# Attention and feed-forward on one core: the add that builds x moves to the next slot, loads run further ahead, and five engines follow a written order

## The chip, the cores and the metric

The kernel runs on one core of a Trainium2 chip. The metric is the device time of one execution in microseconds; lower is better. The profile is that of one execution of its own. Its engines are called PE (TensorE, matmuls), DVE (VectorE), ACT (ScalarE), POOL (GpSimd) and SP (SyncE); the last two issue most of the DMAs.

## The reference

Two layers, one behind the other. The first is attention over q, k, v of shape (8, 8, 576, 64): batches, heads, tokens, head dimension. Each head's output is the sum of a coarse part and a local part:

```python
q_d = q.reshape(B, H, Sd, 4, D).mean(axis=3)        # k_d, v_d likewise
out_d = sm_attn(q_d, k_d, v_d)                      # softmax attention over 144 pooled tokens
out_up = np.repeat(out_d, 4, axis=2)
mask = np.abs(pos[:, None] - pos[None, :]) < 4      # each token sees 3 neighbours on each side
out_local = softmax(where(mask, scale * q @ k.T, -1e9)) @ v
attn_out = out_up + out_local
```

Heads are then put side by side, which gives x with 8 * 576 = 4608 tokens of 512 numbers. The second layer is a gated feed-forward block with d_ff = 1536:

```python
out = (np.maximum(x @ w_gate, 0) * (x @ w_val)) @ w_out
```

Inputs and output are float32 in memory. The kernel converts to float16 while loading and adds up matmuls in float32.

## The kernel before, in words

The work is cut in two ways. Attention goes by **pairs** of heads of one batch: 32 pairs `hp`, four to a batch. Feed-forward goes by **chunks** of 512 tokens: nine chunks `c`. A chunk needs the x of all four pairs of the batches that it touches, so chunk c can be complete once pair 4c+3 is.

A loop over **slots** `s` from -5 to 35 ties the two together. Slot s does attention for pair hp = s + 5 and a quarter of the feed-forward of chunk s // 4: three blocks `emit_h` (128 columns of d_ff each) and, from slot 4 on, one block `emit_y` (128 tokens of output) of the chunk before. Slots below 0 hold attention alone, slots from 28 on almost feed-forward alone. Four more `emit_y` end the program.

The helpers, with what they issue:

- `emit_load(hp)`: POOL issues six DMAs from memory, two each for q, k and v of a pair, into rings of NL = 5 buffers (`q16`, `k16`, `vw`); the first and the last pair have their v in more pieces.
- `emit_wslice`, `emit_wo`: POOL issues slices of the three weight matrices, in slots -4 to 3.
- `emit_qkT(hp)`: SP issues two transposing DMAs, q16 to `qT` and k16 to `kT` (rings of 3).
- `emit_pool(hp)`: two DVE reductions, the sums of four tokens of qT and kT (L179).
- `emit_s1(hp)`: scores on PE (L203 coarse, L218 local), exponentials on ACT (L226, L235), the band masks on DVE (L238).
- `emit_vd(hp)`: pooled v on PE (L188), copied by DVE (L195).
- `emit_s2(hp)`: the products with v on PE (L254, L266), their division by the row sums on DVE (L274 to L285) into `xo`; SP then transposes `xo` to `xoT` by DMA (L291), and DVE adds the coarse part, repeated four times, to the local part and writes `xT` (L292).
- `emit_h(c, jj)`: eight matmuls of 512 columns (L308), Relu on ACT, the product `gT` on DVE (L318). The first four matmuls take one quarter of x each, which is one pair's heads.
- `emit_y(c, ty)`: twelve matmuls (L324), a copy on ACT and the DMA to memory.

All matmul results share one ring of eight PSUM banks. In `with tc.manual_schedule(engines={PE})` only PE follows the program's text as its order. The order of the instructions on DVE, ACT, SP and POOL, their DMAs included, is set ahead of time by a planner from its own cost estimates; each engine then works through its list in order, waiting where an input or a buffer isn't ready. In the trace the planner's list on DVE for a slot is: the add to xT for the pair of the slot before, the masks and the two reductions mixed, the first gT, the output of the next pair, the second gT, the copy of vd, the third gT. On SP the transpose of xo comes first, those of q and k behind it. On POOL it drew some q and k loads ahead of the v loads.

Of the kernel before, what the change touches and what calls it, by code (L numbers as in the profile page):

```python
# [10 lines left out]
FP16 = mybir.dt.float16  # L11
AF = mybir.ActivationFunctionType
ALU = mybir.AluOpType
AX = mybir.AxisListType
PE = mybir.EngineType.PE


def _np_constants():
# [28 lines left out]
def kernel(  # L47
# [44 lines left out]
    def ring(n, shape, dtype, name):  # L92
        return [keep.tile(shape, dtype, name=f"{name}{i}") for i in range(n)]

    NL = 5
    q16 = ring(NL, [96, NB, 128], FP16, "q16_")
    k16 = ring(NL, [96, NB, 128], FP16, "k16_")
    vw = ring(NL, [128, 2, NB, 65], FP16, "vw_")
    qT = ring(3, [128, S], FP16, "qT_")
    kT = ring(3, [128, KW], FP16, "kT_")  # L100
    qd = ring(2, [128, SD], FP16, "qd_")
    kd = ring(2, [128, SD], FP16, "kd_")
    ee = ring(2, [128, 2, S + 32], FP16, "ee_")
    ed = ring(2, [72, 2, 2 * SD + 64], FP16, "ed_")
    vd = ring(2, [72, 2, 2, 65], FP16, "vd_")
    xo = ring(2, [96, NB + 2, 128], FP16, "xo_")
    xoT = ring(2, [128, NB + 2, 96], FP16, "xoT_")
    xT = keep.tile([128, NPB, NTOK], FP16, name="xT")

    for t in kT:  # L110
# [51 lines left out]
                )  # L162

    def emit_qkT(hp):
        r, r3 = hp % NL, hp % 3
        nc.sync.dma_start_transpose(
            out=qT[r3].rearrange("p (j t) -> p j t", j=NB),
            in_=q16[r].rearrange("p j c -> p (j c)"),
        )
        nc.sync.dma_start_transpose(  # L170
            out=kT[r3][:, KPAD : KPAD + S].rearrange("p (j t) -> p j t", j=NB),
            in_=k16[r].rearrange("p j c -> p (j c)"),
        )

    def emit_pool(hp):
        r3, r2 = hp % 3, hp % 2
        with nc.allow_low_precision(reason="4:1 pooling sum"):
            for src, dst in ((qT[r3][:, :], qd[r2]), (kT[r3][:, KPAD : KPAD + S], kd[r2])):
                nc.vector.tensor_reduce(  # L179
                    out=dst, in_=src.rearrange("p (t f) -> p t f", f=4), axis=AX.X, op=ALU.add  # L180
                )
# [13 lines left out]
        nc.vector.tensor_copy(out=vd[hp % 2], in_=ps[0:72, :, :, :])  # L195

    def emit_s1(hp):
        r3, r2 = hp % 3, hp % 2
        sd_ps = [psum.tile([72, 2, SD], FP32, name="sd_ps", tag="bank") for _ in range(2)]
        for c in range(2):  # L200
            for hh in range(2):
                lo = 64 * hh
                nc.tensor.matmul(  # L203
                    out=sd_ps[hh][:, c, :],
                    lhsT=kd[r2][lo : lo + 64, bass.ts(c, 72)],
                    rhs=qd[r2][lo : lo + 64, :],
                    start=True,
                    stop=True,
                )
        sc_ps = []  # L210
        for g in range(2):
            pair = [psum.tile([128, 3, NQ], FP32, name="sc_ps", tag="bank") for _ in range(2)]
            sc_ps.append(pair)
            for jj in range(3):
                j = 3 * g + jj
                for hh in range(2):
                    lo = 64 * hh
                    nc.tensor.matmul(  # L218
                        out=pair[hh][:, jj, :],
                        lhsT=kT[r3][lo : lo + 64, NQ * j + KPAD - 3 : NQ * j + KPAD + 125],  # L220
                        rhs=qT[r3][lo : lo + 64, NQ * j : NQ * j + NQ],
                        start=True,
                        stop=True,
                    )
        for hh in range(2):
            nc.scalar.activation(  # L226
                out=ed[r2][:, hh, 0 : 2 * SD],
                in_=sd_ps[hh].rearrange("p c t -> p (c t)"),
                func=AF.Exp,
                scale=scale / 16.0,  # L230
            )
        for g in range(2):
            for hh in range(2):
                o = ee[r2][:, hh, 288 * g : 288 * g + 288]
                nc.scalar.activation(  # L235
                    out=o, in_=sc_ps[g][hh].rearrange("p j t -> p (j t)"), func=AF.Exp, scale=scale
                )
                nc.vector.tensor_tensor(  # L238
                    out=o,
                    in0=o,  # L240
                    in1=masks_sb[:, 3 * g : 3 * g + 3, :].rearrange("p j t -> p (j t)"),
                    op=ALU.mult,
                )

    def emit_s2(hp):
        r2 = hp % 2
        b, kk = hp // NPB, hp % NPB
        x = xo[r2]
        od = psum.tile([128, 2, 2, 65], FP32, name="od_ps", tag="bank")
        for hh in range(2):  # L250
            for tcx in range(2):
                for c in range(2):
                    s0 = c * SD + 72 * tcx
                    nc.tensor.matmul(  # L254
                        out=od[:, hh, tcx, :],
                        lhsT=ed[r2][:, hh, s0 : s0 + 128],
                        rhs=vd[r2][:, c, hh, :],
                        start=(c == 0),
                        stop=(c == 1),
                    )  # L260
        us = []
        for hh in range(2):
            u = psum.tile([128, NB, 65], FP32, name="u_ps", tag="bank")
            us.append(u)
            for j in range(NB):
                nc.tensor.matmul(  # L266
                    out=u[:, j, :],
                    lhsT=ee[r2][:, hh, NQ * j : NQ * j + 128],
                    rhs=vw[hp % NL][:, hh, j, :],
                    start=True,  # L270
                    stop=True,
                )
        rd = small.tile([72, 2, 2], FP32, name="rd", tag="rd")
        nc.vector.reciprocal(out=rd, in_=od[0:72, :, :, 64])  # L274
        for hh in range(2):
            nc.vector.tensor_tensor(
                out=x[0:72, NB : NB + 2, 64 * hh : 64 * hh + 64],
                in0=od[0:72, hh, :, 0:64],
                in1=_sap(rd, (0, 72), 2 * hh, [[1, 2], [0, 64]]),
                op=ALU.mult,  # L280
            )
        for hh in range(2):
            ru = small.tile([96, NB], FP32, name="ru", tag="ru")
            nc.vector.reciprocal(out=ru, in_=us[hh][0:96, :, 64])
            nc.vector.tensor_tensor(  # L285
                out=x[:, 0:NB, 64 * hh : 64 * hh + 64],
                in0=us[hh][0:96, :, 0:64],
                in1=_sap(ru, (0, 96), 0, [[1, NB], [0, 64]]),
                op=ALU.mult,
            )  # L290
        nc.sync.dma_start_transpose(out=xoT[r2], in_=x.rearrange("p j c -> p (j c)"))  # L291
        nc.vector.tensor_tensor(  # L292
            out=xT[:, kk, b * S : (b + 1) * S].rearrange("p (c t f) -> p c t f", c=2, f=4),
            in0=xoT[r2][:, 0:NB, :].rearrange("p j t -> p (j t)").rearrange(
                "p (c t f) -> p c t f", c=2, f=4
            ),
            in1=_sap(xoT[r2], (0, 128), NB * 96, [[96, 2], [1, 72], [0, 4]]),
            op=ALU.add,
        )
# [37 lines left out]
    def emit_wslice(i):  # L337
        for src, dst in ((moe_w_gate, wg_sb), (moe_w_val, wv_sb)):
            nc.gpsimd.dma_start(
                dst[:, :, 384 * i : 384 * (i + 1)],  # L340
                _dap(src, 384 * i, [[D_FF, 128], [128 * D_FF, 4], [1, 384]]),
            )
# [4 lines left out]
            _dap(moe_w_out, 384 * i * D_MODEL, [[D_MODEL, 128], [128 * D_MODEL, 3], [1, D_MODEL]]),  # L347
        )

    with tc.manual_schedule(engines={PE}):  # L350
        emit_load(0)
        nc.sync.dma_start(masks_sb, masks_dr)
        nc.sync.dma_start(pool_sb, pool_dr)
        emit_load(1)
        emit_load(2)
        emit_qkT(0)
        emit_pool(0)
        for s in range(-LEAD, NCH * 4):
            hp = s + LEAD
            if hp + 3 < NP:  # L360
                emit_load(hp + 3)
            if s < 0:
                if s >= -4:
                    emit_wslice(s + 4)
            elif s < 4:
                emit_wo(s)
            if hp + 1 < NP:
                emit_qkT(hp + 1)
            if hp < NP:
                emit_s1(hp)  # L370
            if s >= 4:
                emit_y(s // 4 - 1, s % 4)
            if hp + 1 < NP:
                emit_pool(hp + 1)
            if s >= 0:
                emit_h(s // 4, 3 * (s % 4))
            if 1 <= hp <= NP:
                emit_s2(hp - 1)
            if s >= 0:
                emit_h(s // 4, 3 * (s % 4) + 1)  # L380
            if hp < NP:
                emit_vd(hp)
            if s >= 0:
                emit_h(s // 4, 3 * (s % 4) + 2)
        for ty in range(4):
            emit_y(NCH - 1, ty)

# [29 lines left out]
```

## Time and profile before

| | |
|---|---|
| median of 3 runs | 424.23 us (422.62 to 426.31) |
| profiled execution | 425.76 us, its span 424.0 us |
| mean granted TensorE clock | 0.987 |
| PE busy | 350.9 us, 83% of the span |
| DVE busy | 229.6 us, 54% |
| ACT busy | 148.0 us, 35% |
| POOL busy | 159.8 us, 38% |
| moved by DMA | 46.36 MB, mean 109 GB/s |

Rows of one digit per slice cut the span into 40 equal parts of 10.6 us; a digit is the busy share in tenths, 9 being 90% or more. A row of the waits reads: engine and line that waited, what it waited for, microseconds in total, number of times, longest. A row of the chain reads: start, duration, what ran; the chain is followed back from the last instruction to whatever released each step. A row of a timeline reads: start, duration, engine, line, operation, output <- inputs, shapes, how many were merged, and in brackets the idle time ahead of it with its releaser. SPq is SP's queue, on which the transposing DMAs are issued; the row's duration there is the issue alone.

### The profile page before, as it was taken

The numbers are of one execution on the slowest core, as the hardware profiler recorded it, in microseconds if no ns is written. First come the engines' busy times: TensorE is split into PE (matmuls) and PEld (weight loads), VectorE is DVE, ScalarE is ACT, GpSimd is POOL, SyncE is SP. The second block draws the span as 40 slices with busy tenths as digits, with TensorE's granted clock in tenths as the row PEclk, the third lists the DMA queues.
The fourth block names the chain that finished last, engine by engine and source line by source line (L and its number), as shares of the span: only waits on it lengthen the run. The fifth ranks groups of instructions, "written<-read, shape, count | busy, mean of one in ns | idle before, by whom it ended". The sixth has DMA issues, their size and how long they took to land.

```text
span 424.0 us, 7217 instructions
## 1 busy us (share of the span) xinstructions
PE 350.9 (83%) x2640; PEld 178.1 (42%) x2640; DVE 229.6 (54%) x588; ACT 148.0 (35%) x337; POOL 159.8 (38%) x229
## 2 busy tenths in 40 slices
PE   0152324977899979997999999999999999999996
PEld 0142212432445535553555445555555544444442
DVE  0364443356677567766777667785876552222320
ACT  1131110432344434443444454444444423323321
POOL 9995656646944444544553544111200000000000
PEclk9999999986999999999999999999999999999999
DMA  8999999999999999999999999869611221001002
GB/s 78 134 173 160 175 171 176 157 156 167 104 155 127 123 130 127 129 124 115 126 132 116 131 122 136 117 105 98 109 45 45 53 54 51 25 26 51 25 26 99
DMA packets 203604, 46.36 MB, mean 109 GB/s; under 512 B 193072, under 2 KB 198960, under 8 KB 203568
## 3 DMA queue, kind: packets, MB, share of 16 engines
q0 software_dynamic: 133584, 20.47, 68.6%
q1 hardware_dynamic: 64800, 15.99, 28.0%
q10 hardware_dynamic: 5184, 9.44, 6.3%
q8 instruction: 21, 0.34, 0.4%
q14 instruction: 15, 0.12, 0.1%
HBM read 41.14 MB, written 9.44 MB: 119 GB/s over the span
## 4 chain that ended last, share of the span: by engine, by line
PE 55%; DMA 26%; DVE 13%; issue 3%; POOL 2%; ACT 0%; DVEq 0%; SPq 0%; POOLq 0%
PE h_ps L308 32%; PE y_ps L324 17%; DMA xoT_109<-xo_107 12%; DMA xoT_108<-xo_106 10%; DVE gT L318 2%; PE u_ps L266 2%; DMA vw_85<-in_v_dram 2%; DVE ee_100 L238 1%; PE vd_ps L188 1%; DMA q_2_77<-in_q_dram 1%; DVE xo_106 L285 1%; DVE xT L292 1%; PE od_ps L254 1%; DMA qT_92<-q_2_77 1%; DVE xo_107 L285 1%
## 5 line engine op out<-in xcount | busy, mean ns | idle before, releaser
L308 PE MATMUL h_ps<-xT,wg_sb 128*128 128x512 f16 x432 | 115.2, 388 | 20.0 <-DVE xT L292 20.0
L308 PE MATMUL h_ps<-xT,wv_sb 128*128 128x512 f16 x432 | 114.1, 387 | 6.1 <-DVE gT L318 6.1
L324 PE MATMUL y_ps<-wo_sb,gT 128*128 128x512 f16 x432 | 98.9, 380 | 0.0
L308 PEld LDWEIGHTS <-wv_sb 128*128 128x128 f16 x432 | 43.0, 100 | 77.3 <-issue 29.4
L324 PEld LDWEIGHTS <-gT 128*128 128x128 f16 x432 | 40.5, 98 | 47.3
L308 PEld LDWEIGHTS <-wg_sb 128*128 128x128 f16 x432 | 39.3, 99 | 42.9 <-issue 6.3
L332 ACT COPY y_sb<-y_ps 128x512 f32<-128x512 f32 x36 | 21.1, 586 | 63.7 <-PE y_ps L324 63.7
L292 DVE TENSOR_TENSOR xT<-xoT_109 128x576 f16<-128x576 f16 x16 | 12.1, 758 | 45.3 <-DMA xoT_109<-xo_107 45.0
L292 DVE TENSOR_TENSOR xT<-xoT_108 128x576 f16<-128x576 f16 x16 | 12.1, 758 | 43.6 <-DMA xoT_108<-xo_106 43.4
L226 ACT ACTIVATE ed_102<-sd_ps 72x288 f16<-72x288 f32 x32 | 11.3, 402 | 36.2 <-PE sd_ps L203 36.2
L235 ACT ACTIVATE ee_101<-sc_ps 128x288 f16<-128x288 f32 x64 | 21.0, 412 | 1.0 <-PE sc_ps L218 1.0
L235 ACT ACTIVATE ee_100<-sc_ps 128x288 f16<-128x288 f32 x64 | 20.7, 413 | 0.0
L226 ACT ACTIVATE ed_103<-sd_ps 72x288 f16<-72x288 f32 x32 | 11.3, 402 | 26.9 <-PE sd_ps L203 26.9
L203 PE MATMUL sd_ps<-qd_96,kd_98 64*72 64x144 f16 x64 | 5.6, 259 | 17.7 <-DVE kd_98 L179 17.7
L128 POOL DMA_DIRECT2D q_0_75<-in_q_dram x14 | 10.5, 760 | 20.8 <-DMA qT_90<-q_0_75 6.5
L285 DVE TENSOR_TENSOR xo_106<-u_ps,ru 96x384 f16<-96x384 f32 x32 | 17.5, 548 | 0.5
L285 DVE TENSOR_TENSOR xo_107<-u_ps,ru 96x384 f16<-96x384 f32 x32 | 17.5, 548 | 0.4
L188 PEld LDWEIGHTS <-pool_sb 128*128 128x128 f16 x192 | 14.6, 104 | 6.5
L128 POOL DMA_DIRECT2D q_1_76<-in_q_dram x14 | 10.3, 742 | 18.5 <-DMA qT_91<-q_1_76 5.4
L238 DVE TENSOR_TENSOR ee_100<-ee_100,masks_sb 128x288 f16<-128x288 f16 x64 | 16.1, 300 | 0.0
L238 DVE TENSOR_TENSOR ee_101<-ee_101,masks_sb 128x288 f16<-128x288 f16 x64 | 16.1, 300 | 0.0
L128 POOL DMA_DIRECT2D q_3_78<-in_q_dram x12 | 8.8, 741 | 18.4 <-DMA qT_92<-q_3_78 6.4
(307 smaller groups left out, 490.7 us busy)
## 6 DMA issues: line engine op xcount, KB each, us to landing
out_dram<-y_sb ACTq DMA_DIRECT2D x36, 256.0 KB, 2.0
wg_sb<-in_moe_w_gate_dram POOLq DMA_DIRECT2D x4, 384.0 KB, 9.7
wv_sb<-in_moe_w_val_dram POOLq DMA_DIRECT2D x4, 384.0 KB, 9.7
wo_sb<-in_moe_w_out_dram POOLq DMA_DIRECT2D x4, 384.0 KB, 9.6
vw_85<-in_v_dram POOLq DMA_DIRECT2D x13, 96.0 KB, 5.9
vw_86<-in_v_dram POOLq DMA_DIRECT2D x13, 96.0 KB, 4.5
vw_87<-in_v_dram POOLq DMA_DIRECT2D x12, 96.0 KB, 4.4
vw_88<-in_v_dram POOLq DMA_DIRECT2D x12, 96.0 KB, 4.3
```

The costliest lines, as they stand in the source:

```text
L128: nc.gpsimd.dma_start(dst[:, :, 64 * hh : 64 * hh + 64], _dap(src, off + hh * S * D, [[D, 96], [NQ * D, NB], [1, D]]),)
L188: nc.tensor.matmul(out=ps[:, c, :, :], lhsT=pool_sb[:, sig, :], rhs=t[:, :, 3 * c + sig, :], start=(sig == 0), stop=(sig == 2),)
L226: nc.scalar.activation(out=ed[r2][:, hh, 0 : 2 * SD], in_=sd_ps[hh].rearrange("p c t -> p (c t)"), func=AF.Exp, scale=scale / 16.0,)
L235: nc.scalar.activation(out=o, in_=sc_ps[g][hh].rearrange("p j t -> p (j t)"), func=AF.Exp, scale=scale)
L238: nc.vector.tensor_tensor(out=o, in0=o, in1=masks_sb[:, 3 * g : 3 * g + 3, :].rearrange("p j t -> p (j t)"), op=ALU.mult,)
L266: nc.tensor.matmul(out=u[:, j, :], lhsT=ee[r2][:, hh, NQ * j : NQ * j + 128], rhs=vw[hp % NL][:, hh, j, :], start=True, stop=True,)
L285: nc.vector.tensor_tensor(out=x[:, 0:NB, 64 * hh : 64 * hh + 64], in0=us[hh][0:96, :, 0:64], in1=_sap(ru, (0, 96), 0, [[1, NB], [0, 64]]), ...
L292: nc.vector.tensor_tensor(out=xT[:, kk, b * S : (b + 1) * S].rearrange("p (c t f) -> p c t f", c=2, f=4), in0=xoT[r2][:, 0:NB, :].rearrang ...
L308: nc.tensor.matmul(out=h, lhsT=w[:, kk, bass.ts(jj, 128)], rhs=xT[:, kk, c * TCH : (c + 1) * TCH], start=(kk == 0), stop=(kk == 3),)
L318: nc.vector.tensor_tensor(out=gt, in0=r1, in1=h2, op=ALU.mult)
L324: nc.tensor.matmul(out=y_ps, lhsT=gts[c, jj][:, bass.ts(ty, 128)], rhs=wo_sb[:, jj, :], start=(jj == 0), stop=(jj == NJJ - 1),)
L332: nc.scalar.copy(out=y_sb, in_=y_ps)
```

## The change

Four things.

1. The add of L292 leaves `emit_s2` for a function of its own, `emit_xadd`, and is emitted one slot later: in slots from 0 on behind the masks and reductions and ahead of the first `emit_h`, in slots below 0 at the slot's end.
2. Loads are emitted four pairs ahead in place of three, q and k transposes two pairs ahead in place of one.
3. Rings grow: q16, k16, vw from 5 to 7, qT and kT from 3 to 4, xo and xoT from 2 to 3.
4. `manual_schedule` takes all five engines, so DVE, ACT, SP and POOL follow the text's order too.

```diff
-    NL = 5
+    NL = 7
-    qT = ring(3, [128, S], FP16, "qT_")
-    kT = ring(3, [128, KW], FP16, "kT_")
+    qT = ring(4, [128, S], FP16, "qT_")
+    kT = ring(4, [128, KW], FP16, "kT_")
-    xo = ring(2, [96, NB + 2, 128], FP16, "xo_")
-    xoT = ring(2, [128, NB + 2, 96], FP16, "xoT_")
+    xo = ring(3, [96, NB + 2, 128], FP16, "xo_")
+    xoT = ring(3, [128, NB + 2, 96], FP16, "xoT_")
...
-        nc.sync.dma_start_transpose(out=xoT[r2], in_=x.rearrange("p j c -> p (j c)"))
+        nc.sync.dma_start_transpose(out=xoT[hp % 3], in_=x.rearrange("p j c -> p (j c)"))
+
+    def emit_xadd(hp):
+        b, kk = hp // NPB, hp % NPB
+        r2 = hp % 3
         nc.vector.tensor_tensor(
             out=xT[:, kk, b * S : (b + 1) * S].rearrange("p (c t f) -> p c t f", c=2, f=4),
...
+    def emit_slot(s):
+        hp = s + LEAD
+        if hp + 4 < NP:
+            emit_load(hp + 4)
+        if s < 0:
+            if s >= -4:
+                emit_wslice(s + 4)
+        elif s < 4:
+            emit_wo(s)
+        if hp + 2 < NP:
+            emit_qkT(hp + 2)
+        if hp < NP:
+            emit_s1(hp)
+        if hp + 1 < NP:
+            emit_pool(hp + 1)
+        if s < 0:
+            if hp >= 1:
+                emit_s2(hp - 1)
+            emit_vd(hp)
+            if hp >= 2:
+                emit_xadd(hp - 2)
+            return
+        if s >= 4:
+            emit_y(s // 4 - 1, s % 4)
+        if hp - 2 < NP:
+            emit_xadd(hp - 2)
+        emit_h(s // 4, 3 * (s % 4))
+        if hp - 1 < NP:
+            emit_s2(hp - 1)
+        emit_h(s // 4, 3 * (s % 4) + 1)
+        if hp < NP:
+            emit_vd(hp)
+        emit_h(s // 4, 3 * (s % 4) + 2)
 
-    with tc.manual_schedule(engines={PE}):
+    with tc.manual_schedule(engines={ET.PE, ET.DVE, ET.Activation, ET.SP, ET.Pool}):
         emit_load(0)
         nc.sync.dma_start(masks_sb, masks_dr)
         nc.sync.dma_start(pool_sb, pool_dr)
         emit_load(1)
+        emit_qkT(0)
         emit_load(2)
-        emit_qkT(0)
+        emit_qkT(1)
         emit_pool(0)
+        emit_load(3)
         for s in range(-LEAD, NCH * 4):
...
-            if hp + 3 < NP:
-                emit_load(hp + 3)
...
-            if hp + 1 < NP:
-                emit_qkT(hp + 1)
...
-            if 1 <= hp <= NP:
-                emit_s2(hp - 1)
...
+            emit_slot(s)
```

The order of PE's instructions is the same in both.

More of the change, by code (lines that the diff above doesn't have):

```diff
@@ L14 @@
 AX = mybir.AxisListType
-PE = mybir.EngineType.PE
+ET = mybir.EngineType
 def _np_constants():
@@ L164, in emit_qkT @@
     def emit_qkT(hp):
-        r, r3 = hp % NL, hp % 3
+        r, r3 = hp % NL, hp % 4
         nc.sync.dma_start_transpose(
@@ L175, in emit_pool @@
     def emit_pool(hp):
-        r3, r2 = hp % 3, hp % 2
+        r3, r2 = hp % 4, hp % 2
         with nc.allow_low_precision(reason="4:1 pooling sum"):
@@ L197, in emit_s1 @@
     def emit_s1(hp):
-        r3, r2 = hp % 3, hp % 2
+        r3, r2 = hp % 4, hp % 2
         sd_ps = [psum.tile([72, 2, SD], FP32, name="sd_ps", tag="bank") for _ in range(2)]
@@ L246, in emit_s2 @@
         r2 = hp % 2
-        b, kk = hp // NPB, hp % NPB
-        x = xo[r2]
+        x = xo[hp % 3]
         od = psum.tile([128, 2, 2, 65], FP32, name="od_ps", tag="bank")
@@ L354 @@
         emit_load(1)
+        emit_qkT(0)
         emit_load(2)
-        emit_qkT(0)
+        emit_qkT(1)
         emit_pool(0)
+        emit_load(3)
         for s in range(-LEAD, NCH * 4):
-            hp = s + LEAD
-            if hp + 3 < NP:
-                emit_load(hp + 3)
[L362 to L366, printed above, removed]
-            if hp + 1 < NP:
-                emit_qkT(hp + 1)
[L369 to L376, printed above, removed]
-            if 1 <= hp <= NP:
-                emit_s2(hp - 1)
[L379 to L384, printed above, removed]
+            emit_slot(s)
         for ty in range(4):
```

## The prediction

> **What bounds the kernel now.** I read the page first: TensorE's busy row by slice, the DMA row, then who waits for whom, then the chain in order of time, then the timelines of the engines at which the chain leaves TensorE.
>
> ```profile
> span 424.0 us, 7217 instructions
> PE   0152324977899979997999999999999999999996
> DMA  8999999999999999999999999869611221001002
> DVE xT L292 <- DMA xoT_109<-xo_107: 45.0, 14, 6.1
> DVE xT L292 <- DMA xoT_108<-xo_106: 43.4, 14, 6.0
> PE h_ps L308 <- DVE xT L292: 20.0, 6, 9.5
> ```
>
> TensorE is full in the second half and nearly empty in the first sixth; VectorE stands 88 us before the add at L292, waiting for the transpose of x. The chain cuts the span into stages:
>
> ```profile
> 29.54 8.61 DMA xoT_108<-xo_106
> 40.54 7.83 DMA xoT_109<-xo_107
> 69.54 2.29 PE h_ps L308 x5
> 117.61 1.24 PE h_ps L308 x5
> 123.78 2.70 PE y_ps L324 x12
> 264.27 2.70 PE y_ps L324 x12
> 273.63 2.70 PE y_ps L324 x12
> 330.50 2.70 PE y_ps L324 x12
> ```
>
> Stage A, to 69.5 us: attention with no feed-forward work. Stage B, 69.5 to 117.6: slots 0 to 3, up to the last weight block of slot 4's first h matmul. Stage C: the rest. An undisturbed slot with y takes 273.63 - 264.27 = 9.36 us, all of it TensorE; without y (2.6) it is 6.8. B should take 4 x 6.8 + 2.6 = 29.8 and takes 48.1: 18.3 lost. In C, the 22 y from 123.78 to 330.50 take 206.7 us where 21 x 9.36 is 196.6: 10.1 lost. Behind that the rows show TensorE without a gap, and the change leaves it alone.
>
> Why A and B lose: VectorE works in order and stops at the add.
>
> ```profile
> 31.85 0.29 DVE L276 TENSOR_TENSOR xo_107<-od_ps,rd 72x128 f16<-72x128 f32 x1
> 38.17 0.76 DVE L292 TENSOR_TENSOR xT<-xoT_108 128x576 f16<-128x576 f16 x1 [6.03 <-DMA xoT_108<-xo_106]
> 38.85 0.28 DVE L276 TENSOR_TENSOR xo_107<-od_ps,rd 72x128 f16<-72x128 f32 x1
> 96.98 0.76 DVE L292 TENSOR_TENSOR xT<-xoT_109 128x576 f16<-128x576 f16 x1 [6.06 <-DMA xoT_109<-xo_107]
> DMA to landing us min/median/max: 2.7/4.6/9.4
> ```
>
> At 31.85 it had begun pair 1's output, and sat 6 us in the middle of it on pair 0's transpose. One round is a transpose, L, plus what VectorE does from the add to the next issue. L is some 8 us beside weight loads, 2.7 with nothing beside it.
>
> **The change, part by part.**
>
> *A: the add leaves the middle of the slot.* Below s = 0 it now ends the slot, for pair hp-2, so two transposes can be in flight. The order differs from 31.85 on. Five more memsets on POOL (0.3 at most each, row below) shift all by about 0.45, an estimate. Pair 1's output needs 40.54 - 38.85 = 1.7 more, so its transpose leaves at 33.5. From then the q and k transposes of the next pairs are the limit; I take 8 us for each transpose in flight here, the 7.83 above. Pair 4's k transpose follows at 33 and lands near 40, so pair 2's output is ready at 42.7. Pair 5's load is now issued at 28.7 to 33.4, lands by 38, is transposed by 46, and pair 3's output is ready at 48.8. Its transpose lands at 56.8; the add takes 0.76. Pair 6's transposes, which the add now stands behind on VectorE, are in by 54.5. First h complete at 57.6, not 69.5: 11.9 us earlier.
>
> *B: weights against the round.* In slots from 0 on the add stands ahead of the first gT and of the output of the next pair, so here one transpose alone is in flight again.
>
> ```profile
> 287.51 0.69 DVE L318 TENSOR_TENSOR gT<-r_3565,h_ps 128x512 f16<-128x512 f16 x1 [0.63 <-PE h_ps L308]
> 289.99 1.21 SPq L291 DMA_TRANSPOSE xoT_109<-xo_107  x1
> 2.12 0.30 POOL L120 MEMSET xo_107<- 32x256 f16 x1
> 28.19 0.79 POOL L339 DMA_DIRECT2D wg_sb<-in_moe_w_gate_dram  x1
> 34.91 0.76 POOL L339 DMA_DIRECT2D wg_sb<-in_moe_w_gate_dram  x1 [0.63 <-DMA wg_sb<-in_moe_w_gate_dram]
> 45.52 0.75 POOL L339 DMA_DIRECT2D wg_sb<-in_moe_w_gate_dram  x1 [0.84 <-DMA wg_sb<-in_moe_w_gate_dram]
> 55.19 0.75 POOL L339 DMA_DIRECT2D wg_sb<-in_moe_w_gate_dram  x1 [0.51 <-DMA wg_sb<-in_moe_w_gate_dram]
> 65.82 0.78 POOL L345 DMA_DIRECT2D wo_sb<-in_moe_w_out_dram  x1
> 74.54 0.75 POOL L345 DMA_DIRECT2D wo_sb<-in_moe_w_out_dram  x1
> 82.57 0.75 POOL L345 DMA_DIRECT2D wo_sb<-in_moe_w_out_dram  x1
> 93.54 1.66 POOL L159 DMA_DIRECT2D vw_86<-in_v_dram  x2 [4.05 <-PE u_ps L266]
> 95.18 0.75 POOL L345 DMA_DIRECT2D wo_sb<-in_moe_w_out_dram  x1
> wo_sb<-in_moe_w_out_dram POOLq DMA_DIRECT2D x4, 384.0 KB, 9.6
> ```
>
> From gT to the issue is 289.99 - 287.51 = 2.5 us; with the add a round is L + 3.2. Four rounds from 56.8 at L = 8.3 (weights are loading throughout) end at 103. That isn't what decides: slot 4's y needs the last slice of wo. POOL issues weights at a pace set by their own landing (each wg waits for the wg before it), and now puts one pair more ahead of each. So the first slice moves from 28.2 to 33.4; at the old steps of 6.7, 10.6, 9.7, 10.6, 8.7 and 8.0, and 8.5 in place of 12.6 since the 4.05 us wait for u goes with seven buffers, the last leaves at 96.2 and lands at 106. Three matmuls of y and three of h (0.22 each) come before the fourth: 107.3. So 10.3 of the 11.9 remain at the end of B.
>
> POOL's and SP's orders change too. SP now issues a q and k transpose ahead of x's, so a late load would hold x's back; pair 7's would be in flight when pair 4's x goes out at 60, which could make that L 10 to 12. The 3 us by which the round beats the weights cover it. The fourth q, k buffer and third x buffer only take waits away.
>
> *C: two opposite terms.* The stalls at the start of a chunk and those between are different things.
>
> ```profile
> 199.65 0.38 PE L308 MATMUL h_ps<-xT,wg_sb 128*128 128x512 f16 x1 [1.88 <-DVE xT L292]
> 282.41 0.32 PE L203 MATMUL sd_ps<-qd_96,kd_98 64*72 64x144 f16 x4
> 283.36 1.30 ACT L235 ACTIVATE ee_100<-sc_ps 128x288 f16<-128x288 f32 x4
> 285.51 1.03 PE L308 MATMUL h_ps<-xT,wg_sb 128*128 128x512 f16 x4
> 286.13 0.74 DVE L179 TENSOR_REDUCE kd_98<-kT_94 128x144 f16<-128x576 f16 x1
> 278.78 1.64 POOL L159 DMA_DIRECT2D vw_89<-in_v_dram  x2 [7.72 <-PE u_ps L266]
> 140.91 1.21 SPq L291 DMA_TRANSPOSE xoT_108<-xo_106  x1
> 147.33 0.76 DVE L292 TENSOR_TENSOR xT<-xoT_108 128x576 f16<-128x576 f16 x1 [4.54 <-DMA xoT_108<-xo_106]
> ```
>
> Each fourth slot's first h reads, in its fourth matmul, the pair added last (the 1.88 above). Before, the add ran ahead of the masks; now it stands behind four masks and two poolings. Counted from the slot's first matmul (282.41): the exponentials end at +2.25, the last mask at +2.6, the poolings at +3.95 (two at 0.66 apart), the add at +4.7; the fourth matmul is due at 285.51 + 0.65, +3.75. So TensorE waits at least 0.95 us at five chunk starts, also at those where it waited for nothing before: **+4.8**, which doesn't depend on L as long as that is below 5.7.
>
> The other stalls are rounds longer than 9.36. With L + 3.2 a round fits while L is below 6.16. In this stage POOL will be held by its v loads, which wait for u as at 278.78, and each release sends a pair's six loads (v, then the next q and k) 2 us ahead of x's transpose. The nearest such case, loads from 2.2 us ahead, is 140.91: landing and add start at 147.33, L = 6.4, the worst of the stage. With nothing beside it L is 2.7. I take 5.3, between the two and nearer the loaded row: these stalls vanish but for some 1.2 us in all. C loses 6.0 in place of 10.1: 4.1 gained.
>
> The Trainium skill ("DMA: Bandwidth & Descriptors", Queues, rings and completion order) speaks against this part: each DMA engine takes turns between the queue rows that have work, packet by packet. Loads that run further ahead keep their row always filled, so x's transpose gets at best every second turn. As an estimate from that rule, L would be 2 x 2.7 = 5.4 beside a steady flow of loads, a round of 8.6, still under 9.36; the trace agrees in size (4.6 median, 6.4 worst beside pair loads, 8 beside weights).
>
> *Sum.* 10.3 + 4.1 = 14.4 us off. The profiled execution took 425.76 us (its span 424.0 and 1.76 around it): 411.4. It lay 1.5 above the median of the three runs, 424.23; on that median it is **410**.
>
> **Rivals.**
>
> *The start is paced by DMA.* For it: the DMA row is at 9 from the second slice on. Faster slots add transposes, and weights move one pair back. If each of the seven weight steps grows by 1.1 us, the last wo lands 7.7 later and A and B keep only 2.6; with C's 4.1 that is 417.5. With B back at 117.6 it is 420. Against: bytes needed by then grow by one load and two transposes' worth only.
>
> *C gains nothing.* The planner had already put the add at the next slot's head, ahead of the masks, which is better for chunk starts. If rounds still exceed 9.36 as often, C loses 10.1 again: 424.23 - 10.3 = 414.
>
> *The weights hold up less.* If they land as they did relative to the pairs, the round decides: 103.6, and with L nearer 6.5 (B's own rows range down to 4.6) 96 to 100. Stalls in C fall to the five chunk starts: 18 + 5 gained, 401.
>
> *Slower: the transpose always lands beside loads.* Place: stage C, the round L + 3.2 on 23 slots. Each us of L above 6.16 costs 23 us. The gains of A and B and all of C's old stalls (20.4) are used up at L = 7.05. At 7.8, as beside weights, it costs 37.7 less 20.4: 441. For it: POOL's release sits just ahead of x's transpose in each slot. Against: no L beside pair loads passed 6.4 in this trace.
>
> **How the numbers follow.** Forecast 0.42, lighter weights 0.18, C gains nothing 0.15, DMA-paced start 0.16, slower 0.09. The range leaves out the slower case and the far end of the lighter weights: 400 to 422. One per cent is 4.2 us, about what a measurement of this kernel tells from no change. Faster by more (below 420): all of forecast, lighter weights and C, and half of the DMA-paced start, 0.81 with a little taken off; the other half and some of the rest within 1%.
>
> **What would show it.** Right: first h near 58 and slot 4's first h near 107, with wo's last landing just ahead of it; VectorE's wait for xoT far below 88 us; h waiting about 1 us for xT at five chunk starts; y spacings of 9.36 between. Wrong: the first weight slice issued at 33 but the last wo after 110; xoT's median landing above 6; y spacings of 10 or more in a row.

## The result: 412.83 us, 2.8% faster

| | before | after |
|---|---|---|
| median | 425.27 us (422.62 to 426.37, 4 runs) | 412.83 us (411.14 to 415.19, 4 runs) |
| profiled execution | 425.76 us, span 424.0 | 413.45 us, span 411.7 |

The ratio is 0.972, with an interval from 0.9649 to 0.9792. Of the profiled execution 12.3 us are gone; the prediction's sum was 14.4.

The profile after, from the page: the span, TensorE's busy tenths in 40 slices, and four rows of who waits for whom (microseconds, times, longest). L295 is the add that was L292, L290 the transpose that was L291, L311 is h and L327 is y.

```profile
span 411.7 us, 7186 instructions
PE   0143429689699999998999999999999999999996
PE h_ps L311 <- DVE xT L295: 13.5, 7, 5.9
DVE xT L295 <- DMA xoT_118<-xo_115: 10.1, 4, 5.3
DVE xT L295 <- DMA xoT_119<-xo_116: 7.6, 2, 4.8
DVE xT L295 <- DMA xoT_117<-xo_114: 5.8, 6, 2.2
```

TensorE's row stands at 9 from the twelfth slice on but for one 8 and the last; before, 7s and 8s went on to the nineteenth. VectorE waits 10.1 + 7.6 + 5.8 = 23.5 us for x's transpose, where it stood 88.4. The same stages in the chain in order of time (start, duration, what ran):

```profile
60.17 2.29 PE h_ps L311 x5
97.96 8.74 DMA wo_sb<-in_moe_w_out_dram
116.78 2.70 PE y_ps L327 x12
318.18 2.70 PE y_ps L327 x12
```

The first complete h comes at 60.17, not 69.54: 9.4 us earlier. The y of slot 5 comes at 116.78, not 123.78: 7.0 earlier, so 2.4 were given back in between. From there the same 22 y take 318.18 - 116.78 = 201.4 us and took 206.7: 5.3 gained. 7.0 + 5.3 = 12.3, the whole difference. Behind that the two traces run alike.

Slot 4 on TensorE, from its timeline, and the add that it waits for, from VectorE's; then one window of 5 us over all engines (busy time of PE, PEld, DVE, ACT and POOL with counts, then granted clock, DMA share, GB/s):

```profile
106.75 1.44 PE L327 MATMUL y_ps<-wo_sb,gT 128*128 128x512 f16 x3 [4.24 <-DMA wo_sb<-in_moe_w_out_dram]
107.98 1.94 PE L311 MATMUL h_ps<-xT,wg_sb 128*128 128x512 f16 x4
109.71 1.91 PE L311 MATMUL h_ps<-xT,wv_sb 128*128 128x512 f16 x4
112.32 1.02 PE L311 MATMUL h_ps<-xT,wg_sb 128*128 128x512 f16 x4
108.52 0.76 DVE L295 TENSOR_TENSOR xT<-xoT_118 128x576 f16<-128x576 f16 x1 [5.27 <-DMA xoT_118<-xo_115]
105.00:110.00 5.00, 3.25 (x8) 1.09 (x8) 0.76 (x1) 0.63 (x2) 2.37 (x4) 0.52 1.66 146
```

Two things come within some 2.5 us of each other: the last slice of wo at 106.75, and the add's end at 108.52 + 0.76 = 109.28, which the fourth matmul of h needs. Before, h stood at that matmul until 117.61: 8.3 us are gained there. And TensorE, after 4.24 us of waiting, works at half pace: four matmuls take 1.9 us at a granted clock of 0.52, and 1.02 again from 112.32. From the fourth matmul to the next y takes 7.5 us (109.28 to 116.78), and took 6.2 before (117.61 to 123.78). So 1.3 of the 8.3 are lost again.

### The profile page after: what moved, and what is told of

Same layout as the page of the kernel before. It is cut to its first block, busy times and chain, and to the rows that moved or that the text cites. A ratio compares the mean times of both kernels' runs of the same rounds, so it can differ in the third digit from the quotient of the medians.

```text
span 411.7 us, 7186 instructions
## 1 busy us (share of the span) xinstructions
PE 350.3 (85%) x2640; PEld 178.2 (43%) x2640; DVE 244.3 (59%) x588; ACT 147.9 (36%) x337; POOL 160.2 (39%) x234
## 4 chain that ended last, share of the span: by engine, by line
PE 71%; DMA 16%; DVE 7%; POOL 2%; ACT 1%; issue 1%; SPq 0%; DVEq 0%; POOLq 0%
PE h_ps L311 42%; PE y_ps L327 20%; DMA xoT_117<-xo_114 4%; PE u_ps L265 3%; DMA xoT_118<-xo_115 2%; DMA wo_sb<-in_moe_w_out_dram 2%; PE vd_ps L188 2%; DMA kT_101<-k_5_87 2%; DMA xoT_119<-xo_116 2%; PE od_ps L253 2%; DMA vw_89<-in_v_dram 2%; PE sd_ps L203 1%; DMA kT_102<-k_2_84 1%; DVE ee_109 L238 1%; PE sc_ps L218 1%; DMA k_2_84<-in_k_dram 1%
## 5 line engine op out<-in xcount | busy, mean ns | idle before, releaser
L311 PE MATMUL h_ps<-xT,wg_sb 128*128 128x512 f16 x432 | 115.8, 389 | 13.5 <-DVE xT L295 13.5
L311 PE MATMUL h_ps<-xT,wv_sb 128*128 128x512 f16 x432 | 114.4, 388 | 0.0
L327 PE MATMUL y_ps<-wo_sb,gT 128*128 128x512 f16 x432 | 99.7, 381 | 4.2 <-DMA wo_sb<-in_moe_w_out_dram 4.2
L311 PEld LDWEIGHTS <-wv_sb 128*128 128x128 f16 x432 | 43.0, 99 | 64.7 <-issue 16.1
L327 PEld LDWEIGHTS <-gT 128*128 128x128 f16 x432 | 40.4, 98 | 51.9 <-issue 4.8
L311 PEld LDWEIGHTS <-wg_sb 128*128 128x128 f16 x432 | 39.5, 99 | 43.2 <-issue 7.0
L203 PE MATMUL sd_ps<-qd_104,kd_106 64*72 64x144 f16 x64 | 5.7, 253 | 22.8 <-DVE kd_106 L179 22.4
L238 DVE TENSOR_TENSOR ee_108<-ee_108,masks_sb 128x288 f16<-128x288 f16 x64 | 18.5, 307 | 7.9 <-ACT ee_108 L235 7.9
L238 DVE TENSOR_TENSOR ee_109<-ee_109,masks_sb 128x288 f16<-128x288 f16 x64 | 18.3, 307 | 6.9 <-ACT ee_109 L235 6.9
L203 PEld LDWEIGHTS <-kd_106 64*72 64x72 f16 x64 | 2.6, 115 | 29.0 <-DVE kd_106 L179 22.9
L203 PE MATMUL sd_ps<-qd_105,kd_107 64*72 64x144 f16 x64 | 5.7, 253 | 10.2 <-DVE kd_107 L179 7.9
L295 DVE TENSOR_TENSOR xT<-xoT_118 128x576 f16<-128x576 f16 x11 | 8.3, 754 | 10.1 <-DMA xoT_118<-xo_115 10.1
L179 DVE TENSOR_REDUCE qd_104<-qT_96 128x144 f16<-128x576 f16 x8 | 6.0, 748 | 13.1 <-DMA qT_96<-q_0_75 13.0
L159 POOL DMA_DIRECT2D vw_91<-in_v_dram x10 | 8.3, 833 | 14.0 <-PE u_ps L265 12.2
L159 POOL DMA_DIRECT2D vw_92<-in_v_dram x9 | 7.5, 843 | 15.3 <-PE u_ps L265 15.3
L284 DVE TENSOR_TENSOR xo_114<-u_ps,ru 96x384 f16<-96x384 f32 x22 | 12.2, 554 | 0.8
```

What stands on the lines that cost most here:

```text
L159: nc.gpsimd.dma_start(t[:, hh, :, 0:64], _dap(v, base + hh * S * D, [[D, 128], [NQ * D, NB], [1, D]]),)
L203: nc.tensor.matmul(out=sd_ps[hh][:, c, :], lhsT=kd[r2][lo : lo + 64, bass.ts(c, 72)], rhs=qd[r2][lo : lo + 64, :], start=True, stop=True,)
L238: nc.vector.tensor_tensor(out=o, in0=o, in1=masks_sb[:, 3 * g : 3 * g + 3, :].rearrange("p j t -> p (j t)"), op=ALU.mult,)
L284: nc.vector.tensor_tensor(out=x[:, 0:NB, 64 * hh : 64 * hh + 64], in0=us[hh][0:96, :, 0:64], in1=_sap(ru, (0, 96), 0, [[1, NB], [0, 64]]), ...
L295: nc.vector.tensor_tensor(out=xT[:, kk, b * S : (b + 1) * S].rearrange("p (c t f) -> p c t f", c=2, f=4), in0=xoT[r2][:, 0:NB, :].rearrang ...
L311: nc.tensor.matmul(out=h, lhsT=w[:, kk, bass.ts(jj, 128)], rhs=xT[:, kk, c * TCH : (c + 1) * TCH], start=(kk == 0), stop=(kk == 3),)
```

## The experiments

My theory: the gain is the round (transpose, add, output of the next pair) taken off VectorE's path. That takes the add's new place, the written order that keeps it there, and the lead of the q and k transposes. Weights set how long A and B still last; the place of the add behind masks and poolings sets the rest of C's loss.

**1. The planner sets the order again, with all else as after.**

```diff
-    with tc.manual_schedule(engines={ET.PE, ET.DVE, ET.Activation, ET.SP, ET.Pool}):
+    with tc.manual_schedule(engines={ET.PE}):
```

> Only the written order is undone: the planner again orders VectorE, ScalarE, SyncE and GpSimd; the later add, the leads and the larger rings stay. Theory (the add's place on VectorE and two transposes in flight make the gain, whoever writes the order): if the planner leaves the add behind the reductions, within 1% of the changed kernel, 409 to 417 us, VectorE's wait for xoT under 35 us. If it draws the add ahead of the masks again, as it did before, a round is L + 5.4 again, VectorE waits 60 us or more for xoT, and the time is 417 to 423. Rival (the written order makes the gain): 424 in either case.

Measured: 424.8 us beside 428.34 of before, ratio 0.9934 (0.99 to 0.9969). VectorE's timeline in a slot of stage C, and its wait over the span:

```profile
158.39 0.76 DVE L295 TENSOR_TENSOR xT<-xoT 128x576 f16<-128x576 f16 x1 [3.57 <-DMA xoT<-xo]
159.07 0.52 DVE L238 TENSOR_TENSOR ee<-ee,masks_sb 128x288 f16<-128x288 f16 x2
DVE xT L295 <- DMA xoT<-xo: 72.8, 32, 5.9
```

The planner puts the add ahead of the masks again, though the text now has it behind them, and the wait stays. This is the second branch of the expectation. The time lies above its 417 to 423, but the kernel before was slower here too; as ratios of 424.23 they are 0.983 to 0.997, and the measured ratio lies within. The wait is over 60 us, and the interval leaves out a ratio of 1, the rival's 424. All the rest of the change without the order is worth 0.7% of the 2.8%.

**2. The written order, with the add right behind its own pair's output.**

```diff
             if hp >= 1:
                 emit_s2(hp - 1)
+                emit_xadd(hp - 1)
             emit_vd(hp)
-            if hp >= 2:
-                emit_xadd(hp - 2)
...
-        if hp - 2 < NP:
-            emit_xadd(hp - 2)
...
         if hp - 1 < NP:
             emit_s2(hp - 1)
+            emit_xadd(hp - 1)
```

> Only the move of the add is undone: it follows its own pair's output at once, in the written order, with the leads and rings of the change. Theory: VectorE then stands still for the whole transpose, and a round is L plus all of VectorE's slot, about L + 7.0. With L = 5.4 a slot of stage C takes 12.4 in place of 9.36 us: 23 x 3.0 = 70 us more, 470 to 490 us; with L = 4 about 450. VectorE's wait for xoT 110 to 150 us. Rival (buffers and leads make the gain, the add's place does not matter): 411 to 418.

Measured: 470.81 us, ratio 1.1001 (1.0923 to 1.1079). From its waits:

```profile
DVE xT L295 <- DMA xoT<-xo: 142.9, 32, 8.5
```

Every pair's add now waits, 142.9 / 32 = 4.5 us on average, since nothing stands between it and its transpose. The time lies at the lower end of the 470 to 490 expected. The written order without the later add does harm; with it comes the gain.

**3. Leads and rings of before, with the new order.** NL, the rings of qT and kT, and both emission distances go back.

```diff
-    NL = 7
+    NL = 5
-    qT = ring(4, [128, S], FP16, "qT_")
+    qT = ring(3, [128, S], FP16, "qT_")
...
-        if hp + 4 < NP:
-            emit_load(hp + 4)
+        if hp + 3 < NP:
+            emit_load(hp + 3)
...
-        if hp + 2 < NP:
-            emit_qkT(hp + 2)
+        if hp + 1 < NP:
+            emit_qkT(hp + 1)
```

> Only the leads and rings of loads and of the q and k transposes are undone (three pairs and one pair ahead, 5 and 3 buffers); the add's place, the written order and the three x buffers stay. Theory (they matter in the first 110 us alone): a pair's transposes now leave behind the x transpose of the slot before and are needed in their own slot, so the first complete h is 3 to 8 us later than 60.2; the last wo leaves one load earlier but POOL waits for u again, so it lands within 4 us of 106.7. From slot 4 on nothing changes but L. In all 413 to 421. Rival (the leads make the gain): 422 to 427. Rival (loads further ahead cost time beside the x transpose): under 409, with L below 5 in stage C.

Measured: 464.84 us, ratio 1.0863 (1.0785 to 1.0942). My expectation, 413 to 421, was off by over 40 us, and the rival's 422 to 427 by nearly as much. SP's and VectorE's timelines and the waits:

```profile
204.24 1.21 SPq L290 DMA_TRANSPOSE xoT<-xo  x1
205.62 1.25 SPq L166 DMA_TRANSPOSE qT<-q  x1
211.30 0.75 DVE L179 TENSOR_REDUCE qd<-qT 128x144 f16<-128x576 f16 x1 [3.54 <-DMA qT<-q]
215.99 1.21 SPq L290 DMA_TRANSPOSE xoT<-xo  x1
DVE qd L179 <- DMA qT<-q: 112.3, 31, 13.0
```

In the written order the poolings of a pair come in the slot in which its transposes were issued, behind x's. A slot is then the transposes' latency plus VectorE's work, 215.99 - 204.24 = 11.75 us: the old round with q in x's place.

**4. Which of the two leads it is.** Only the loads go back (NL = 5, three pairs ahead); the q and k transposes stay two ahead.

> The changed kernel with the loads three pairs ahead and five buffers again, while the q and k transposes stay two ahead with four buffers. My theory: of the leads only that of the q and k transposes is needed by the written order, because there the poolings stand in the slot in which the transposes would otherwise still be under way; the loads land two slots early in either case. So near the changed kernel, 412 to 419 us, and VectorE's wait for qT and kT stays under 15 us. Rival: the loads' lead is what counts (a load that lands late holds the q and k transposes and with them SP's whole queue): 430 to 465 us, with the waits on qT back at 50 to 110 us.

Measured: 416.13 us (415.82 to 417.27), ratio 0.9757 (0.9714 to 0.9801), beside 413.77 (412.85 to 415.17) of the changed kernel on the same chip. VectorE's wait for qT:

```profile
DVE qd L179 <- DMA qT<-q: 21.8, 5, 12.0
```

The wait was expected under 15, but 12.0 of the 21.8 are the one at the start. The lead of the q and k transposes makes nearly all the difference between the ratios 1.0863 and 0.97; that of the loads some 2 us, at the edge of what can be told. No run takes back the third buffer of xo and xoT alone, so what it is worth stays open.

**5. No weights to load.** VectorE fills wg_sb, wv_sb and wo_sb with a constant ahead of everything, and no weight is read from memory, so the output isn't the layer's.

```diff
+    for t in (wg_sb, wv_sb, wo_sb):
+        nc.vector.memset(t, 0.02)
...
-        if s < 0:
-            if s >= -4:
-                emit_wslice(s + 4)
-        elif s < 4:
-            emit_wo(s)
```

> Leaves out all twelve weight loads; VectorE fills the weights with a constant at the start. Theory (in A and B the x transpose is slow beside weight loads, and the round it belongs to is the bound): L is 4 to 6 there in place of 8.5 to 9.8, the first complete h comes at 48 to 53 in place of 60.2, a round is L + 3.4, so slot 4's last weight block of the first h comes 36 to 40 later, at 86 to 92, not 109.3; in all 389 to 397. Rival (loads of pairs, not weights, slow the start): first h at 58 or later, in all 405 or more.

Measured, one execution: 399.82 us, span 398.1. From SP's timeline, x's transpose for pairs 0 and 3, with pair 3's add from VectorE's; then the first h from the chain, and the matmul of slot 4 that waits for the add:

```profile
31.68 1.21 SPq L292 DMA_TRANSPOSE xoT<-xo  x1
49.75 1.22 SPq L292 DMA_TRANSPOSE xoT<-xo  x1
56.59 0.76 DVE L297 TENSOR_TENSOR xT<-xoT 128x576 f16<-128x576 f16 x1 [1.46 <-DMA xoT<-xo]
57.40 2.29 PE h_ps L313 x5
96.77 0.38 PE L313 MATMUL h_ps<-xT,wg_sb 128*128 128x512 f16 x1 [1.22 <-DVE xT L297]
```

The fills are a flaw: pair 0's transpose leaves 2.3 us later than in the changed kernel (29.43 there, its row is quoted in the next section). Counted from it, the first h comes 25.7 us later here and 30.7 there; from the first h to slot 4's fourth matmul 39.4 here and 49.1 there. So by this count weights cost A 5.0 and B 9.7 us. The first h, slot 4's matmul and the time come 3 to 5 us behind the theory's ranges, 2.3 of it by the fills; the rival's 58 and 405 aren't reached either. Pair 3's transpose still takes 56.59 - 49.75 = 6.8 us with no weights. Pair loads and the other transposes are what is left beside it, and no run separates the two.

**6. Short transposes in stage C.** Loads stop with pair 13; later pairs compute with the data left in the buffers, so the output differs.

```diff
-        if hp + 4 < NP:
+        if hp + 4 < 14:
```

> Leaves out all loads of pairs 14 to 31, so later pairs compute with old data. Theory (in C the x transpose takes 5.4 because the loads released by u lie beside it, and the chunk starts wait for the add's place, not for the transpose): L falls to 2.8 to 3.2 from about slot 6 on, while TensorE's five waits stay at 0.7 each and slots at 9.36, so the time stays within 1% of the changed kernel. Rival (the chunk starts wait for the transpose): the waits go, 4 us less; rival (L = 5.4 comes from the q and k transposes behind it or the output DMA): L stays above 5.

Measured, one execution: 413.09 us, span 411.2, beside 413.77. The time from issue to landing of x's transpose, of the changed kernel and of this one, and then of this one the first of five such waits at chunk starts:

```profile
DMA to landing us min/median/max: 2.8/4.9/9.8
```

```profile
DMA to landing us min/median/max: 2.8/2.9/10.4
148.97 0.38 PE L311 MATMUL h_ps<-xT,wg_sb 128*128 128x512 f16 x1 [0.71 <-DVE xT L295]
```

The transpose is 2 us shorter and the time moves by 0.7 us. Four of the five waits stay at 0.70 or 0.71; the fifth, 1.24 us in the changed kernel, falls to 0.70. So in C the transpose is off the path but for that one place, and the rest of the waits are those of the add's place on VectorE.

**7. The newest quarter of x last.** In the first h of a chunk the two matmuls that read the pair added last come after the other six. All of the layer is computed.

```diff
-        for w, h in ((wg_sb, h1), (wv_sb, h2)):
-            for kk in range(4):
+        steps = [(w, h, kk) for w, h in ((wg_sb, h1), (wv_sb, h2)) for kk in range(4)]
+        if jj == 0:
+            steps.sort(key=lambda st: st[2] == 3)
+        for w, h, kk in steps:
```

> The changed kernel, but in the first h of a slot the two matmuls that read the newest quarter of x come last of eight in place of fourth and eighth. Theory (the chunk starts wait because the add stands behind masks and reductions on VectorE, not for the transpose): the matmul is due 0.65 us later, so the five waits of 0.71 fall to 0.1 to 0.2 each and the y spacings of 10.23 to about 9.6: 2.5 to 4 us less, 409 to 410.5. Rival (TensorE's records only show the wait where it is easiest to see, and it comes back at the next block): spacings stay 10.2, 413.

Measured on one chip: 413.23 us, ratio 0.9653 (0.9585 to 0.972), too wide to tell it from the change. On another it ran beside the changed kernel.

> The changed kernel again, for its ratio on the chip of the next three: 0.965 to 0.975 of the kernel before.

> The order with the two matmuls of the newest quarter last, again, beside the changed kernel on one chip. Theory (chunk starts wait for the add's place on VectorE): 2.5 to 4 us under the changed kernel, the waits of TensorE for xT in stage C 0.1 to 0.2 us each. Rival: no difference, y spacings of 10.2 at chunk starts.

Measured: the changed kernel 413.77 us, ratio 0.9704 (0.9652 to 0.9757); newest last 410.03 us, ratio 0.9614 (0.9563 to 0.9664). The 3.7 us lie in the upper part of what was expected. The intervals overlap, but five of its six executions took 409.07 to 410.57 us and all six of the changed kernel 412.85 to 415.17. A chunk start from the next experiment's kernel, which holds the same edit:

```profile
150.06 0.38 PE L313 MATMUL h_ps<-xT,wg_sb 128*128 128x512 f16 x1
```

Six matmuls cover the add, and the matmul that needs it no longer shows a wait. So it is at four of the five chunk starts; the fifth still waits 0.80 us, behind an add that x's transpose held for 0.64. This version beats both kernels.

**8. wo ahead of the pair loads of its slot, alone and with newest last.**

```diff
+        if 0 <= s < 4:
+            emit_wo(s)
         if hp + 4 < NP:
             emit_load(hp + 4)
-        if s < 0:
-            if s >= -4:
-                emit_wslice(s + 4)
-        elif s < 4:
-            emit_wo(s)
+        if -4 <= s < 0:
+            emit_wslice(s + 4)
```

> The changed kernel with each piece of wo issued ahead of the pair loads of its slot instead of behind them. My theory: the last piece lands some 2 to 4 us earlier, y of slot 4 no longer waits for it (4.24 us in the changed kernel), but the add that the first h of chunk 1 waits for comes from the x round (108.5 us) and not from wo, so the time falls by 0.5 to 2 us only, to a ratio 0.966 to 0.970. Rival: wo sets the end of this stretch, and the whole wait goes: 4 to 5 us, a ratio of 0.959 to 0.961.

> Both edits: the newest quarter of x last in the first h of a chunk, and wo ahead of the pair loads. Newest last alone had a ratio of 0.9614. The y of slot 4 waits less for wo, six of the first eight h matmuls of chunk 1 are done before the add: 1 to 3 us below newest last alone, a ratio of 0.954 to 0.959. If the wo edit is worth nothing: 0.961.

Measured: alone 414.86 us (414.35 to 417.85), ratio 0.974 (0.9698 to 0.9782); with newest last 410.14, ratio 0.9601 (0.9556 to 0.9646). From the timeline of the first:

```profile
102.28 2.75 PE L327 MATMUL y_ps<-wo_sb,gT 128*128 128x512 f16 x12 [0.19 <-ACT ed L226]
108.91 0.59 PE L311 MATMUL h_ps<-xT,wg_sb 128*128 128x512 f16 x1 [3.24 <-DVE xT L295]
```

The wait for wo is gone, and h waits for the add instead, until 108.91. No gain shows, alone (a ratio of 0.974 beside 0.9704) or with newest last (0.9601 beside 0.9614): the round sets the end of B, and wo only nearly did. Neither my 0.5 to 2 us alone nor the 1 to 3 us for both edits can be seen, and the rival's 4 to 5 fall.

**9. A warm TensorE at slot 4.** The kernel with both edits, and between the six matmuls and the two that wait, sixteen whose result nobody reads.

```diff
+                if i == 6 and (c, jj) == (1, 0):
+                    d = psum.tile([128, TCH], FP32, name="d_ps", tag="bank")
+                    for _ in range(16):
+                        nc.tensor.matmul(out=d, lhsT=wg_sb[:, 0, 0:128],
+                                         rhs=xT[:, 0, 0:TCH], start=True, stop=True)
```

> The kernel with both edits, and in the first h of chunk 1, between the six matmuls that are ready and the two that wait for the add, sixteen matmuls whose result nobody reads (128x128 by 128x512, about 4.1 us at a full clock). If the clock that is granted after TensorE's wait there costs the time that I read out of the trace (h x4 at 1.9 us instead of 1.02, some 1.3 us in all), the kernel gains 0.8 to 1.5 us on the one with both edits (a ratio lower by 0.002 to 0.004), and the granted clock between 105 and 115 us is above 0.9. Rival: the x round that follows sets the pace there, so a warm clock gives nothing (ratio the same), or the sixteen matmuls last beyond the add's end and cost up to 2 us.

Measured: 410.94 us (408.39 to 414.36), ratio 0.9637 (0.9586 to 0.9687). TensorE's timeline without the sixteen:

```profile
110.78 0.38 PE L313 MATMUL h_ps<-xT,wg_sb 128*128 128x512 f16 x1 [3.40 <-DVE xT L295]
112.11 1.90 PE L313 MATMUL h_ps<-xT,wg_sb 128*128 128x512 f16 x4
117.87 2.76 PE L329 MATMUL y_ps<-wo_sb,gT 128*128 128x512 f16 x12
```

and with them, and the window from 110 to 115 us:

```profile
104.89 3.62 PE L316 MATMUL d_ps<-xT,wg_sb 128*128 128x512 f16 x16
108.34 0.38 PE L323 MATMUL h_ps<-xT,wg_sb 128*128 128x512 f16 x1
109.40 1.02 PE L323 MATMUL h_ps<-xT,wg_sb 128*128 128x512 f16 x4
113.80 2.76 PE L339 MATMUL y_ps<-wo_sb,gT 128*128 128x512 f16 x12
110.00:115.00 5.00, 5.00 (x42) 2.55 (x41) 3.90 (x13) 2.55 (x7) 4.40 (x6) 1.00 2.08 162
```

That window's granted clock is 1.00 and was 0.66 without the sixteen; from 105 to 110 it is 1.00 in both. Four matmuls take 1.02 us in place of 1.90, and from the waiting matmul to the next y takes 5.46 us in place of 7.09: in the trace the idle wait's price is real, 1.6 us. In the time it doesn't show: the medians differ by 0.8 us the other way, within intervals of some 2 us to either side, so the 0.8 to 1.5 us that I expected are not borne out. Whether the 1.6 us reach the end stays open.

## Why the prediction was right, step by step

**The time.** 412.83 lies in the range, 2.8 above the number; faster by more than 1%, as the chances had it.

**A: right mechanism, two terms mis-sized.** x's transposes of pairs 0 to 3, from SP's timeline, and from VectorE's the last pooling of pair 6, pair 3's add and the product behind it:

```profile
29.43 1.22 SPq L290 DMA_TRANSPOSE xoT_117<-xo_114  x1
34.92 1.23 SPq L290 DMA_TRANSPOSE xoT_118<-xo_115  x1
43.07 1.21 SPq L290 DMA_TRANSPOSE xoT_119<-xo_116  x1
49.84 2.87 SPq L290 DMA_TRANSPOSE xoT_117<-xo_114  x1
57.77 0.75 DVE L179 TENSOR_REDUCE kd_106<-kT_102 128x144 f16<-128x576 f16 x1 [0.69 <-DMA kT_102<-k_6_88]
59.36 0.76 DVE L295 TENSOR_TENSOR xT<-xoT_117 128x576 f16<-128x576 f16 x1 [0.84 <-DMA xoT_117<-xo_114]
62.57 0.69 DVE L321 TENSOR_TENSOR gT<-r_630,h_ps 128x512 f16<-128x512 f16 x1 [2.45 <-PE h_ps L311]
```

Predicted were 33.5, 42.7 and 48.8 for pairs 1 to 3, and 56.8 for the add. Pair 3 left 1.0 late, and L of its transpose, taken as 8, measured 59.36 - 49.84 = 9.5. The 7.83 that I took came from a trace in which at most one of x's was under way. The excess is about that of the issue's own row, 2.87 us where the other three have 1.2. In experiment 5, without weights, the row has 1.22 and L is 6.8. But a shorter L alone would have gained at most 0.84 us: pair 6's transposes, put at 54.5, held VectorE until 57.77, so it came to the add only at 58.52, and x's transpose held it from there to 59.36. A gained 9.4, not 11.9.

**B: the end right to 2 us, its cause named wrongly.** The last wo was predicted to leave at 96.2 and land at 106; it left at 97.96, and y had it at 106.75. But the round was to be done 3 us ahead of wo, at 103, and ended behind it, at 109.28. From SP's and VectorE's timelines, the first of the four transposes of B and its add, the next issue, and the last issue, whose add is the 108.52 above:

```profile
65.27 1.21 SPq L290 DMA_TRANSPOSE xoT_118<-xo_115  x1
75.00 0.76 DVE L295 TENSOR_TENSOR xT<-xoT_118 128x576 f16<-128x576 f16 x1 [3.34 <-DMA xoT_118<-xo_115]
78.37 1.22 SPq L290 DMA_TRANSPOSE xoT_119<-xo_116  x1
99.56 1.22 SPq L290 DMA_TRANSPOSE xoT_118<-xo_115  x1
```

L was 75.00 - 65.27 = 9.7 in the first and 108.52 - 99.56 = 9.0 in the last of them, and over the four 8.3, the number taken. From add to next issue takes 78.37 - 75.00 = 3.4, as good as the 3.2. What failed is the start: the add at the end of A is 2.6 late, and from it to the first issue takes 65.27 - 59.36 = 5.9, not 3.2. In slot 0 the first h can run only behind the add, so the first gT waits 2.45 us for it (the row at 62.57) and the output behind gT too; the sum used the steady round there. Together 5.3 us, and the cover was 3. Experiment 8 shows that the round decides. That the end is right to 2 us is in part luck: the bound that was priced, wo, lies close to the one that decided.

**The half pace of TensorE was in no term.** It is the 1.3 us at slot 4, and about 1 us of the 2.45 (the chain's row of the first h has 2.29 us for five matmuls, that of slot 4 before the change 1.24). The Trainium skill has it ("TensorE: Matmul & The Clock Gate", Part 1: The HAM clock gate): after an idle window of about 3.4 us the array's clock is halved. The trace agrees in two places, waits of 5.9 us (the longest of h for xT) and 4.24, then matmuls at half pace, and experiment 9 takes it away by filling the wait. But half pace comes without such a wait too: from 79.32 on four matmuls of h take 1.89 us, and the longest wait in the 5 us ahead of them is 1.88 us, with four below 0.5 us behind it. And the granted clock of the window from 60 to 65 us reads 1.00, though four matmuls from 60.55 on take 1.91 us. So what wait it takes, this case doesn't settle.

**C: both terms right, the gain a little better.** The other stalls vanish, as forecast: the spacings are 9.36 but for five chunk starts, four of 10.23 and one of 10.75. Those lose 4 x 0.87 + 1.39 = 4.9 us in all, and 6.0 was predicted (five of 0.95, and 1.2 besides). The wait is 0.71 (once 1.24) in place of 0.95. From the chain, two y with one more and a chunk start between them, 19.58 us apart, that is 2 x 9.36 + 0.86; from TensorE's timeline two of the waits:

```profile
250.94 2.70 PE y_ps L327 x12
270.52 2.70 PE y_ps L327 x12
148.91 0.38 PE L311 MATMUL h_ps<-xT,wg_sb 128*128 128x512 f16 x1 [0.71 <-DVE xT L295]
187.75 0.38 PE L311 MATMUL h_ps<-xT,wg_sb 128*128 128x512 f16 x1 [1.24 <-DVE xT L295]
```

"Doesn't depend on L as long as that is below 5.7" is shown by experiment 6 for the four. At the fifth, 187.75, the chain has x's transpose ahead of the add with 5.88 us, just above that limit, and VectorE waited 0.44 for it. That the rest is the add's place is shown by experiment 7, which earns 3.7 us by going round it.

**A step that was wrong and didn't show.** "The fourth q, k buffer and third x buffer only take waits away." The lead of the q and k transposes does far more: without it the written order is 9% slower than before (experiment 3). I costed it at nothing, from a trace in which, behind the start, x's transpose was the only one that held VectorE for long.

**The rivals.** The DMA-paced start needed the seven weight steps to grow by 1.1 us each. The first four grew by 5.1 us in all, but the last three were 2.8 us shorter than put, and the first slice left 0.5 early. So the last wo left only 1.8 us behind the forecast and landed 0.7 behind it: errors that offset each other, and not a sum that was right term by term. "C gains nothing" gives 414, near the measured number, by a mechanism that the spacings refute: C gained 5.3. Lighter weights: they held up as long as forecast. Slower, by transposes over 7.05 in C: the median is 4.9, and with 2.9 (experiment 6) the time is the same within 1 us. What came nearest to the slower side isn't among them: the same place, 465 us, by q's transpose instead of x's.

## What to carry to other kernels

An in-order engine that meets a DMA's latency in every round loses it in every round; move the consumer behind work that doesn't need it, and check each other DMA that the new order reads, since the latency moves to whichever has the shortest lead. When two arrivals fall within the error of their estimates, price both as the bound. Where a wait remains at the head of a chunk, reorder the consumer so that it reads the newest data last: that was worth 3.7 us here, where an earlier wo was worth nothing that shows.

## What the runs showed of the hardware that I had not expected

- Waits of 4.24 and 5.9 us on TensorE are followed by some us at half pace (1.91 us for four matmuls, 1.02 otherwise), and so is a group of shorter waits, the longest 1.88.
- x's transpose takes 2.8 to 2.9 us with no loads beside it and 4.8 (median from 110 to 310 us) beside pair loads in C. In A, pair 3's takes 6.8 with no weights in flight and 9.5 with them.
- In experiment 5 the fill of 128x6144 numbers on VectorE has a row of 5.18 us, but the three begin 6.4 us apart (2.10, 8.51 and 14.92), with 1.23 us of idle time shown between: its row is less than what a fill costs there.
